# Cosformer attention and a quick-GELU MLP on one core: the first batch's chunks 0 and 1 get numerators in single PSUM banks, and w_in's first part comes as two tiles

## The chip, the core and the metric

One core of one Trainium2 chip runs the kernel. The metric is the device time of one execution in microseconds (us), the lower the better. PE is the matmul engine (TensorE; PEld are its weight loads), DVE VectorE, ACT ScalarE, POOL GpSimd, SP the sync engine. SBUF is the on-chip memory of 128 partitions, PSUM the matmul accumulator with eight banks of 512 float32 per partition.

## What is computed

Eight batches of eight heads, 576 positions and head size 64 go through a linear attention; its result, as 4608 tokens of 512 features, goes through an MLP with 2048 hidden features. All inputs are float32.

```python
phi(x) = concat([relu(x) * cos_w, relu(x) * sin_w], -1)   # 64 -> 128 features
kv  = einsum('bhsf,bhsd->bhfd', phi(k), v);  z = sum_s phi(k)
num = einsum('bhsf,bhfd->bhsd', phi(q), kv)
den = einsum('bhsf,bhf->bhs', phi(q), z) + 1e-06
x   = (num / den) as [B*S, H*D]
h   = x @ w_in;   g = h / (1 + exp(-1.702 * h));   out = g @ w_out
```

## The kernel before

The order of work on each engine is the order of the program text. Tiles come from pools, and a tile that takes over a buffer waits for the last reader of the one before it. Two PSUM pools share the eight banks: `pmm`, four single banks (name `mm`), and `pat`, two pairs of banks (name `at`). Everything below is batch 0, up to line 435; the loop over batches 1 to 7 (line 510) and the end are not touched.

**Loads.** SP loads k and q of batch 0 (lines 62 and 63). All others are issued by POOL in one queue, with a cast to bfloat16 where the tile has that type: v of batch 0 in two parts (line 132), the first two quarters of w_in (`load_win`, line 124), after POOL's own share of q the other two, then k of batch 1, two quarters of w_out (`load_wout`, line 127), q and v of batch 1 and the rest of w_out. A quarter of w_in is a tile of 512 hidden features in which feature block `fc` takes every fourth column (line 112); w_out's rows are loaded in the matching order.

**Attention of batch 0.** `trig` (line 135) makes phi of k and q on DVE, ACT and POOL. `ksum` sums phi(k) on PE, so that z is there early. `qturn_pe` (line 167) transposes phi(q) on PE into a `pmm` bank, two blocks of 64 positions at a time, and `qevac` (line 174) copies it to `qT`, on DVE or ACT. `kv_mm` (line 202) forms kv for two head pairs at a time in a `pat` pair, `kv_evac` copies it to `kvs`. Per chunk of 128 positions (four whole chunks and a half one, chunk 4) there follow:

- `num_mm` (line 226): eight matmuls, one per head, 65 columns each (64 numerators and a denominator), into a `pat` pair;
- `num_div` (line 248): DVE adds 1e-6 to the denominators, takes the reciprocal (`inv_of`) and multiplies (line 254, tile `xn`). Chunk 0 has its denominators earlier, from `den_early` (line 241) in a `pmm` bank;
- `xturn_mm` (line 269): PE transposes `xn` in four pieces into free columns of the same `pat` pair;
- `xturn_evac` (line 276): ACT copies that to `xT`, and the pair is free again.

**First product of batch 0.** `mm1_part` (line 291) multiplies w_in's block `fc` with some columns of `xT` into a `pmm` bank. For blocks 0 to 3 this is done chunk by chunk (`part`, line 414: four matmuls of 128 columns per chunk and block, "quarters" below), so that PE can begin while later chunks are still divided. After the last quarter ACT applies the four GELUs, and block 4 on runs on all 512 columns (`mm1`, line 303). The order written out by hand is lines 393 to 435: transposes of pair 3, numerators of chunks 0 and 1, transposes of pair 4, one matmul on zeros (`idle`, line 342), chunk 0's transposes, chunk 2's numerators, chunk 1's transposes, chunk 0's quarters, chunk 3's numerators, chunk 2's transposes, chunk 1's quarters, chunk 4's numerators, chunk 3's transposes, and the quarters of chunks 2 and 3. Since `pat` has two pairs, chunk 2's numerators wait for the copy of chunk 0, chunk 3's for that of chunk 1, and so on.

Of the kernel before, what the change touches and what calls it, by code (L numbers as in the profile page):

```python
# [9 lines left out]
F32 = mybir.dt.float32  # L10
BF16 = mybir.dt.bfloat16
AF = mybir.ActivationFunctionType
MUL = mybir.AluOpType.mult
# [6 lines left out]
def kernel(  # L20
# [9 lines left out]
    nc = tc.nc  # L30
    B, H, S, D = q.shape
    d_model = H * D
    d_ff = moe_w_in.shape[1]
    KC = d_model // 128
# [6 lines left out]
    one = ctx.enter_context(tc.tile_pool(name="one", bufs=1))  # L41
# [3 lines left out]
    small = ctx.enter_context(tc.tile_pool(name="small", bufs=3))  # L45
    pmm = ctx.enter_context(tc.tile_pool(name="pmm", bufs=4, space=PSUM))
# [24 lines left out]
    ident = const.tile([128, 128], BF16)  # L71
# [26 lines left out]
    qn0 = qn.rearrange("p c h f -> p (c h f)")[:, 0:NS * NI * 128].rearrange(  # L98
        "p (j i f) -> p j i f", j=NS, i=NI)
    qT = one.tile([128, H, 640], BF16, name="qT")  # L100
    w_in_sb = [one.tile([128, KC, 512], BF16, name=f"w_in{g}") for g in range(4)]
    w_out_sb = one.tile([128, FC, d_model], BF16, name="w_out_sb")
    nc.gpsimd.memset(vt[:, :, :, 64:66], 1.0)
    nc.gpsimd.memset(qT[:, :, S:640], 0.0)
# [1 line left out]

    win_r = moe_w_in.rearrange("(kc p) f -> p kc f", p=128)
    wout_r = moe_w_out.rearrange("(g p c) d -> p g c d", p=128, c=4)
    w_in_v = [t.rearrange("p k (f c) -> p k c f", c=4) for t in w_in_sb]

    def w_in_of(kc, fc):
        return w_in_v[fc // 4][:, kc, fc % 4, :]

    def load(t, src, b, eng=nc.gpsimd):
        eng.dma_start(out=t, in_=src_of(src, b))
# [5 lines left out]
                            in_=q[b, :, 512:S, :].rearrange("h p d -> p h d"))  # L121

    def load_win(g):
        nc.gpsimd.dma_start(out=w_in_sb[g], in_=win_r[:, :, ts(g, 512)])

    def load_wout(g):
        nc.gpsimd.dma_start(out=w_out_sb[:, ts(g, 4), :], in_=wout_r[:, g])

    gate = const.tile([1, 4], F32)
    nc.gpsimd.tensor_copy(gate[0:1, 0:1], kf[0:1, 0, 0:1])  # L130
    for i in (0, 2):
        nc.gpsimd.dma_start(out=vb[:, i:i + 2], in_=src_of(v, 0, i, i + 2))
    load_win(0)
    load_win(1)
    def trig(dst, src, j, act=False, eng=nc.vector):
        i = src[:, :, ts(j, 64)]
# [30 lines left out]
    def qturn_pe(c, home=None):  # L167
        tp = pmm.tile([128, 2, NI, 128], BF16, name="mm") if home is None else home
        for j in range(2 * c, min(2 * c + 2, NS)):
            for i in range(NI):  # L170
                nc.tensor.transpose(tp[:, j % 2, i], qn0[:, j, i, :], ident)  # L171
        tps[c] = tp

    def qevac(c, act=False):
        n = min(2 * c + 2, NS) - 2 * c
        o = qT[:, :, ds(c * 128, n * 64)].rearrange("f h (j p) -> f j h p", j=n)
        i = tps.pop(c)[:, 0:n].rearrange("f j i (hh p) -> f j (i hh) p", hh=2)
        if act:
            nc.scalar.activation(o, i, AF.Copy)  # L179
        else:  # L180
            nc.vector.tensor_copy(o, i)  # L181
# [10 lines left out]
    st = {}  # L192
# [9 lines left out]
    def kv_mm(i0, i1, rhs, col, n):  # L202
        for i in range(i0, i1):
            for j in range(NS):
                for hh in range(2):
                    r = slice(hh * 64, hh * 64 + 64)
                    nc.tensor.matmul(st["kv", i][:, hh, ds(col, n)], kr[r, j, i, :], rhs(r, i, j),  # L207
                                     start=(j == 0), stop=(j == NS - 1))

    def kv_evac(i0, i1, n=65):  # L210
        o = st["kvs"][:, :, i0:i1, 0:n]
        nc.vector.tensor_copy(o, st["ps", i0].rearrange("p hh (i e) -> p hh i e", e=65)[:, :, :, 0:n])  # L212
# [11 lines left out]
    nums = {}  # L224

    def num_mm(c):
        ps = pat.tile([128, 2, 512], F32, name="at")
        for h in range(H):
            i, hh = divmod(h, 2)
            nc.tensor.matmul(ps[:, h // 4, ds((h % 4) * 65, 65)], qT[:, h, ts(c, 128)],  # L230
                             st["kvs"][:, hh, i, 0:65], start=True, stop=True)
        nums[c] = [ps]

    def inv_of(d):
        den = small.tile([128, 2, 4], F32, name="den")
        nc.vector.tensor_scalar(den, d, 1e-6, None, op0=ADD)  # L236
        inv = small.tile([128, 2, 4], F32, name="inv")
        nc.vector.reciprocal(inv, den)
        return inv

    def den_early(c):
        d = pmm.tile([128, 2, 4], F32, name="mm")
        for h in range(H):
            nc.tensor.matmul(d[:, h // 4, h % 4:h % 4 + 1], qT[:, h, ts(c, 128)],
                             st["kvs"][:, h % 2, h // 2, 64:65], start=True, stop=True)
        return inv_of(d)

    def num_div(c, inv=None):
        ps = nums[c][0]
        pv = ps[:, :, 0:260].rearrange("p a (h e) -> p a h e", h=4)  # L250
        if inv is None:
            inv = inv_of(pv[:, :, :, 64])
        xn = small.tile([128, 2, 4, 64], BF16, name="xn", bufs=4)
        nc.vector.tensor_tensor(xn, pv[:, :, :, 0:64],  # L254
                                inv.unsqueeze(3).to_broadcast([128, 2, 4, 64]), op=MUL)
        nums[c].append(xn)
# [6 lines left out]
    def x_open(b):  # L263
        x[b] = xpool.tile([128, KC, MT], BF16, name="xT")

    def x_of(b, c):
        return xt[:, :, ts(b, 64)] if c == 4 else x[b][:, :, ts(c, 128)]

    def xturn_mm(c):
        ps, xn = nums[c]  # L270
        xv = xn.rearrange("p a h e -> p (a h e)")
        for kc in range(KC):
            o = ps[:, kc // 2, ds(264 + (kc % 2) * 64, 64)].bitcast(BF16)
            nc.tensor.transpose(o, xv[:, ts(kc, 128)], ident)  # L274

    def xturn_evac(b, c):
        ps = nums.pop(c)[0]
        i = ps[:, :, 264:392].bitcast(BF16).rearrange("p a (k t) -> p a k t", k=2)
        o = x_of(b, c).rearrange("p (a k) t -> p a k t", a=2)
        nc.scalar.activation(o, i, AF.Copy)  # L280

    def xturn_dma(b, c):
        xn = nums.pop(c)[1]
        n = 128 if c < 4 else 64
        nc.sync.dma_start_transpose(out=x_of(b, c), in_=xn[0:n].rearrange("p a h e -> p (a h e)"))
# [5 lines left out]
    def mm1_part(b, fc, t0, t1):  # L291
        if t0 == 0:
            hp[fc] = pmm.tile([128, MT], F32, name="mm")
        for kc in range(KC):
            nc.tensor.matmul(hp[fc][:, t0:t1], w_in_of(kc, fc), x[b][:, kc, t0:t1],  # L295
                             start=(kc == 0), stop=(kc == KC - 1))
# [12 lines left out]
    def mm1_tails(fc):  # L309
        hps = pmm.tile([128, NT], F32, name="mm")  # L310
        for kc in range(KC):
            nc.tensor.matmul(hps, w_in_of(kc, fc), xt[:, kc, :], start=(kc == 0), stop=(kc == KC - 1))  # L312
        nc.scalar.activation(gl_t[:, fc, :], hps, AF.Gelu_apprx_sigmoid)  # L313
# [28 lines left out]
    def idle(n, w=None):  # L342
        if w is None:
            w = pmm.tile([128, 512], F32, name="mm")
        for _ in range(n):
            nc.tensor.matmul(w, warm[:, 0:128], warm, start=True, stop=True)
        return w
# [34 lines left out]
    trig(qn0, qf0, 8, eng=nc.gpsimd)  # L382
    nc.gpsimd.tensor_copy(gate[0:1, 1:2], vb[0:1, 3, 0:1])
    load_win(2)
    load_win(3)
    kv_mm(0, 2, vb_rhs, 0, 64)
# [4 lines left out]
    qevac(1)  # L391
    qevac(2, act=True)
    inv0 = den_early(0)
    kv_evac(0, 2, 64)
    kv_mm(2, 4, vb_rhs, 0, 64)
    kv_evac(2, 4, 64)
    qturn_pe(3)
    qevac(3, act=True)
    num_mm(0)
    num_div(0, inv0)  # L400
    num_mm(1)
    num_div(1)
    qturn_pe(4)
    qevac(4)
    idle(1)
    x_open(0)
    xturn_mm(0)
    xturn_evac(0, 0)
    num_mm(2)
    num_div(2)  # L410
    xturn_mm(1)
    xturn_evac(0, 1)

    def part(c, *fcs):
        for fc in fcs:
            mm1_part(0, fc, c * 128, c * 128 + 128)

    part(0, 0, 1, 2, 3)
    num_mm(3)
    num_div(3)  # L420
    xturn_mm(2)
    xturn_evac(0, 2)
    part(1, 0, 1, 2, 3)
    num_mm(4)
    num_div(4)
    xturn_mm(3)
    xturn_evac(0, 3)
    xturn_dma(0, 4)
    part(2, 0, 1, 2)
    part(3, 0, 1)  # L430
    part(2, 3)
    part(3, 2, 3)
# [4 lines left out]

    load(kf, k, 1)
    load_wout(0)
    load_wout(1)  # L440
    load(qf0, q, 1)
    load(vf, v, 1)
    load_wout(2)
    load_wout(3)
    for j in range(NS):
# [137 lines left out]
```

## Time and profile before

| | us |
|---|---|
| median of 3 runs | 291.81 (291.69 to 292.36) |
| profiled execution | 292.75 |
| its span, first to last instruction | 291.0 |
| PE busy in the span | 281.8 |
| PE busy from 0 to 14 us | 10.94 of 14.00 |
| PE busy from 14.0 to 21.7 us | 6.68 of 7.70 |
| PE busy from 21.7 to 32.0 us | 10.25 of 10.30 |

The profiled execution's time is its span and 1.75 us around it. Times in what follows are us from the start of the span. In the chain of waits a row is the start, the duration and the work that the end is owed to, followed back from the last instruction; "issue" is time for which no wait shows. In a timeline a row is start, busy time, engine, line, operation, tiles, shapes and count, and in brackets the engine's idle time before it with what ended it. A matmul's duration includes its way through the array, so matmuls that follow one another start closer together than they are long; what PE is worth is read from the starts. Two views that the next section does not show: PE's waits between 13.7 and 22 us, and a table of durations there.

```profile
PEld L230 <- issue: 0.8, 1, 0.8
PE at L230 <- ACT xT L280: 0.7, 1, 0.7
PEld L274 <- DVE xn L254: 0.4, 1, 0.4
```

```profile
L254 DVE TENSOR_TENSOR xn<-at,inv 128x512 bf16<-128x512 f32 x5 | 3.5, 691 | 0.5 <-PE at L230 0.4
L280 ACT ACTIVATE xT<-at 128x512 bf16<-128x512 bf16 x4 | 2.4, 597 | 2.7 <-PE at L274 2.7
L179 ACT ACTIVATE qT<-mm 128x1024 bf16<-128x1024 bf16 x2 | 2.0, 1023 | 0.9 <-PE mm L171 0.9
```

The first lists what waited for what, in total, how often and the longest; the second gives counts, the busy sum and the mean in ns.

### The profile page before, as it was taken

What the parts mean: (1) busy time and instruction counts of PE and PEld (TensorE: products, weight loads), DVE (VectorE), ACT (ScalarE), POOL (GpSimd) and SP (SyncE); (2) the same over time, 40 slices, a digit from 0 to 9 for tenths busy, and PEclk for the clock granted to TensorE, in tenths of its full rate; (3) what the DMA queues carried; (4) which work ended last, traced back from release to release, by engine and by line L of the source; (5) the groups of instructions that cost most, each with busy time, mean ns of one, the idle gap of its engine ahead of it and who ended that gap; (6) DMA issues with size and microseconds to landing.
All of it is one profiled execution on the core that took longest, in us unless ns stands there. A gap on an engine that the chain in (4) does not pass through costs nothing.

```text
span 291.0 us, 5656 instructions
## 1 busy us (share of the span) xinstructions
PE 281.8 (97%) x2247; PEld 153.0 (53%) x2282; DVE 123.7 (43%) x356; ACT 133.1 (46%) x232; POOL 37.8 (13%) x71
## 2 busy tenths in 40 slices
PE   6989999999999999999999999999999999999995
PEld 2685475555555555555455545554555455544444
DVE  3872656912657354826582567156624200000000
ACT  6857564793157214721463136412651176751111
POOL 6560042301210011001100110011000100002000
PEclk9999999999999999999999999999999999999999
DMA  7999999982699877989797579846952600002322
GB/s 239 247 213 289 368 247 362 239 193 76 128 271 260 219 131 260 289 184 147 221 314 198 96 203 346 222 102 159 373 94 72 119 36 1 0 2 44 84 90 72
DMA packets 67770, 52.48 MB, mean 180 GB/s; under 512 B 47968, under 2 KB 57952, under 8 KB 67744
## 3 DMA queue, kind: packets, MB, share of 16 engines
q1 hardware_dynamic: 60320, 32.52, 47.0%
q0 software_dynamic: 7424, 19.60, 23.9%
q8 instruction: 18, 0.29, 0.4%
q14 instruction: 8, 0.07, 0.1%
HBM read 36.70 MB, written 9.44 MB: 159 GB/s over the span
## 4 chain that ended last, share of the span: by engine, by line
PE 91%; DMA 3%; ACT 2%; DVE 1%; issue 1%; SPq 1%; ACTq 0%
PE mm L332 42%; PE mm L295 37%; PE mm L312 5%; PE at L230 3%; PE at L207 3%; DMA qf<-in_q_dram 3%; ACT g L300 1%; PE at L274 1%; DVE qn L142 1%; DVE qT L181 0%; PE at L171 0%; ACT qT L179 0%; SPq L62 0%; DVE xn L254 0%; ACT xT L280 0%
## 5 line engine op out<-in xcount | busy, mean ns | idle before, releaser
L332 PE MATMUL mm<-w_out_sb,g 128*128 128x512 bf16 (+1 forms) x506 | 116.7, 372 | 1.3 <-issue 0.2
L295 PE MATMUL mm<-xT,w_in 128*128 128x512 bf16 (+1 forms) x551 | 111.9, 360 | 0.5
L300 ACT ACTIVATE g<-mm 128x512 bf16<-128x512 f32 x128 | 75.6, 598 | 31.0 <-PE mm L295 31.0
L295 PEld LDWEIGHTS <-w_in 128*128 128x128 bf16 x560 | 59.8, 113 | 50.9
L332 PEld LDWEIGHTS <-g 128*128 128x128 bf16 x528 | 48.6, 98 | 49.1
L336 ACT ACTIVATE ysb<-mm 128x512 f32<-128x512 f32 (+1 forms) x37 | 21.7, 586 | 105.9 <-PE mm L332 103.0
L340 POOL DMA_DIRECT2D out_dram<-ysb x39 | 21.3, 547 | 204.7 <-ACT ysb L336 204.7
L142 DVE TENSOR_SCALAR kr<-kf,cosw 128x256 bf16<-128x256 f32 x64 | 22.6, 353 | 29.4 <-DMA kf<-in_k_dram 29.4
L254 DVE TENSOR_TENSOR xn<-at,inv 128x512 bf16<-128x512 f32 x40 | 27.7, 691 | 1.9 <-PE at L230 0.4
L142 DVE TENSOR_SCALAR kr<-kf,sinw 128x256 bf16<-128x256 f32 x64 | 22.2, 347 | 0.0
L212 DVE CAST kvs<-at 128x520 bf16<-128x520 f32 (+1 forms) x9 | 5.6, 634 | 33.7 <-PE at L207 33.7
L236 DVE TENSOR_SCALAR den<-at 128x8 f32<-128x8 f32 x39 | 6.5, 166 | 31.4 <-PE at L230 31.4
L230 PEld LDWEIGHTS <-qT 128*128 128x128 bf16 x320 | 14.8, 97 | 8.8 <-issue 0.8
L230 PE MATMUL at<-kvs,qT 128*128 128x65 bf16 x320 | 16.1, 193 | 0.7 <-ACT xT L280 0.7
L155 DVE TENSOR_SCALAR qn<-qf,sinw 128x512 bf16<-128x512 f32 (+1 forms) x30 | 14.4, 480 | 0.0
L155 DVE TENSOR_SCALAR qn<-qf,cosw 128x512 bf16<-128x512 f32 (+1 forms) x30 | 14.3, 476 | 0.0
L312 PE MATMUL mm<-xt,w_in 128*128 128x512 bf16 x63 | 13.9, 379 | 0.1
L332 PE MATMUL mm<-w_out_sb,gl_t 128*128 128x512 bf16 x63 | 13.9, 379 | 0.1
L313 ACT ACTIVATE gl_t<-mm 128x512 bf16<-128x512 f32 x16 | 9.6, 597 | 4.2 <-PE mm L312 4.2
L207 PEld LDWEIGHTS <-kr 64*128 64x128 bf16 x576 | 9.3, 94 | 2.8 <-issue 2.5
L312 PEld LDWEIGHTS <-w_in 128*128 128x128 bf16 x64 | 7.2, 113 | 6.6
L332 PEld LDWEIGHTS <-gl_t 128*128 128x128 bf16 x64 | 6.3, 98 | 7.5
(63 smaller groups left out, 114.5 us busy)
## 6 DMA issues: line engine op xcount, KB each, us to landing
kf<-in_k_dram SPq DMA_DIRECT2D x5, 1152.0 KB, 6.7
vf<-in_v_dram SPq DMA_DIRECT2D x5, 1152.0 KB, 9.5
qf<-in_q_dram SPq DMA_DIRECT2D x5, 1024.0 KB, 5.9
out_dram<-ysb POOLq DMA_DIRECT2D x20, 256.0 KB, 3.9
out_dram<-ysb POOLq DMA_DIRECT2D x19, 128.0 KB, 3.2
kf<-in_k_dram POOLq DMA_DIRECT2D x2, 1152.0 KB, 11.3
vf<-in_v_dram POOLq DMA_DIRECT2D x2, 1152.0 KB, 15.7
w_in<-in_moe_w_in_dram POOLq DMA_DIRECT2D x4, 512.0 KB, 9.5
```

The costliest lines, as they stand in the source:

```text
L142: eng.tensor_scalar(o, i, 0.0, w[:, j:j + 1], op0=MAX, op1=MUL)
L155: nc.vector.tensor_scalar(o, i, 0.0, sc, op0=MAX, op1=MUL)
L207: nc.tensor.matmul(st["kv", i][:, hh, ds(col, n)], kr[r, j, i, :], rhs(r, i, j), start=(j == 0), stop=(j == NS - 1))
L230: nc.tensor.matmul(ps[:, h // 4, ds((h % 4) * 65, 65)], qT[:, h, ts(c, 128)], st["kvs"][:, hh, i, 0:65], start=True, stop=True)
L254: nc.vector.tensor_tensor(xn, pv[:, :, :, 0:64], inv.unsqueeze(3).to_broadcast([128, 2, 4, 64]), op=MUL)
L295: nc.tensor.matmul(hp[fc][:, t0:t1], w_in_of(kc, fc), x[b][:, kc, t0:t1], start=(kc == 0), stop=(kc == KC - 1))
L300: nc.scalar.activation(g, hp.pop(fc), AF.Gelu_apprx_sigmoid)
L312: nc.tensor.matmul(hps, w_in_of(kc, fc), xt[:, kc, :], start=(kc == 0), stop=(kc == KC - 1))
L313: nc.scalar.activation(gl_t[:, fc, :], hps, AF.Gelu_apprx_sigmoid)
L332: nc.tensor.matmul(yp[t, c0][:, c0:c1], w, w_out_sb[:, fc, c0:c1], start=(fc == 0), stop=(fc == FC - 1))
L336: nc.scalar.activation(ysb[:, c0:c1], yp[t, c0][:, c0:c1], AF.Identity)
L340: eng.dma_start(out=dst[:, c0:c1], in_=ysb[p0:p0 + n, c0:c1])
```

## The change

Chunks 0 and 1 have their denominators from `den_early` in one shared `pmm` bank, and their numerators, 64 columns per head, in a `pmm` bank each (`num1_mm`). DVE divides the two one behind the other (`num1_div`), PE transposes the quotients into the front half of the same bank (`x1turn_mm`) and ACT copies them from there (`x1turn_evac`). Chunks 2 and 3 so find both `pat` pairs free after kv, and their numerators come before the transposes of chunks 0 and 1. The matmul on zeros goes, the copy of pair 4 moves from DVE to ACT behind chunk 1's copy, and the quarters are interleaved otherwise: each two blocks of a chunk stand between the transposes of the chunks behind. The first quarter of w_in is two tiles of 256 columns with a DMA each, in which a block takes every second column; the first quarter of w_out is loaded in the row order that this asks for, in pieces of two rows instead of four.

```diff
@@ -98,7 +98,8 @@
     qn0 = qn.rearrange("p c h f -> p (c h f)")[:, 0:NS * NI * 128].rearrange(
         "p (j i f) -> p j i f", j=NS, i=NI)
     qT = one.tile([128, H, 640], BF16, name="qT")
-    w_in_sb = [one.tile([128, KC, 512], BF16, name=f"w_in{g}") for g in range(4)]
+    w_in0 = [one.tile([128, KC, 256], BF16, name=f"w_in0{u}") for u in "ab"]
+    w_in_sb = [one.tile([128, KC, 512], BF16, name=f"w_in{g}") for g in range(1, 4)]
     w_out_sb = one.tile([128, FC, d_model], BF16, name="w_out_sb")
     nc.gpsimd.memset(vt[:, :, :, 64:66], 1.0)
     nc.gpsimd.memset(qT[:, :, S:640], 0.0)
@@ -106,10 +107,14 @@
 
     win_r = moe_w_in.rearrange("(kc p) f -> p kc f", p=128)
     wout_r = moe_w_out.rearrange("(g p c) d -> p g c d", p=128, c=4)
+    wout0_r = moe_w_out[0:512].rearrange("(u p c) d -> p u c d", u=2, c=2)
+    w_in0_v = [t.rearrange("p k (f c) -> p k c f", c=2) for t in w_in0]
     w_in_v = [t.rearrange("p k (f c) -> p k c f", c=4) for t in w_in_sb]
 
     def w_in_of(kc, fc):
-        return w_in_v[fc // 4][:, kc, fc % 4, :]
+        if fc < 4:
+            return w_in0_v[fc // 2][:, kc, fc % 2, :]
+        return w_in_v[fc // 4 - 1][:, kc, fc % 4, :]
 
     def load(t, src, b, eng=nc.gpsimd):
         eng.dma_start(out=t, in_=src_of(src, b))
@@ -121,10 +126,17 @@
                             in_=q[b, :, 512:S, :].rearrange("h p d -> p h d"))
 
     def load_win(g):
-        nc.gpsimd.dma_start(out=w_in_sb[g], in_=win_r[:, :, ts(g, 512)])
+        if g == 0:
+            for u in range(2):
+                nc.gpsimd.dma_start(out=w_in0[u], in_=win_r[:, :, ts(u, 256)])
+        else:
+            nc.gpsimd.dma_start(out=w_in_sb[g - 1], in_=win_r[:, :, ts(g, 512)])
 
     def load_wout(g):
-        nc.gpsimd.dma_start(out=w_out_sb[:, ts(g, 4), :], in_=wout_r[:, g])
+        if g == 0:
+            nc.gpsimd.dma_start(out=w_out_sb[:, 0:4, :].rearrange("p (u c) d -> p u c d", u=2), in_=wout0_r)
+        else:
+            nc.gpsimd.dma_start(out=w_out_sb[:, ts(g, 4), :], in_=wout_r[:, g])
 
     gate = const.tile([1, 4], F32)
     nc.gpsimd.tensor_copy(gate[0:1, 0:1], kf[0:1, 0, 0:1])
@@ -239,11 +251,34 @@
         return inv
 
     def den_early(c):
-        d = pmm.tile([128, 2, 4], F32, name="mm")
+        if c == 0:
+            st["den"] = pmm.tile([128, 2, 2, 4], F32, name="mm")
+        d = st["den"][:, c]
         for h in range(H):
             nc.tensor.matmul(d[:, h // 4, h % 4:h % 4 + 1], qT[:, h, ts(c, 128)],
                              st["kvs"][:, h % 2, h // 2, 64:65], start=True, stop=True)
         return inv_of(d)
+
+    def num1_mm(c):
+        st["n", c] = pmm.tile([128, 512], F32, name="mm")
+        for h in range(H):
+            nc.tensor.matmul(st["n", c][:, ts(h, 64)], qT[:, h, ts(c, 128)],
+                             st["kvs"][:, h % 2, h // 2, 0:64], start=True, stop=True)
+
+    def num1_div(c, inv):
+        xn = small.tile([128, 2, 4, 64], BF16, name="xn", bufs=4)
+        nc.vector.tensor_tensor(xn, st["n", c].rearrange("p (a h e) -> p a h e", a=2, h=4),
+                                inv.unsqueeze(3).to_broadcast([128, 2, 4, 64]), op=MUL)
+        nums[c] = xn
+
+    def x1turn_mm(c):
+        xv = nums.pop(c).rearrange("p a h e -> p (a h e)")
+        for kc in range(KC):
+            nc.tensor.transpose(st["n", c][:, ts(kc, 64)].bitcast(BF16), xv[:, ts(kc, 128)], ident)
+
+    def x1turn_evac(b, c):
+        i = st["n", c][:, 0:256].bitcast(BF16).rearrange("p (k t) -> p k t", k=KC)
+        nc.scalar.activation(x_of(b, c), i, AF.Copy)
 
     def num_div(c, inv=None):
         ps = nums[c][0]
@@ -394,39 +429,43 @@
     kv_evac(0, 2, 64)
     kv_mm(2, 4, vb_rhs, 0, 64)
     kv_evac(2, 4, 64)
+    inv1 = den_early(1)
     qturn_pe(3)
     qevac(3, act=True)
-    num_mm(0)
-    num_div(0, inv0)
-    num_mm(1)
-    num_div(1)
-    qturn_pe(4)
-    qevac(4)
-    idle(1)
-    x_open(0)
-    xturn_mm(0)
-    xturn_evac(0, 0)
+    num1_mm(0)
+    num1_mm(1)
+    num1_div(0, inv0)
+    num1_div(1, inv1)
     num_mm(2)
     num_div(2)
-    xturn_mm(1)
-    xturn_evac(0, 1)
+    qturn_pe(4)
+    x_open(0)
+    x1turn_mm(0)
+    x1turn_evac(0, 0)
+    num_mm(3)
+    num_div(3)
+    x1turn_mm(1)
+    x1turn_evac(0, 1)
+    qevac(4, act=True)
 
     def part(c, *fcs):
         for fc in fcs:
             mm1_part(0, fc, c * 128, c * 128 + 128)
 
-    part(0, 0, 1, 2, 3)
-    num_mm(3)
-    num_div(3)
+    part(0, 0, 1)
+    part(1, 0, 1)
+    part(0, 2)
     xturn_mm(2)
     xturn_evac(0, 2)
-    part(1, 0, 1, 2, 3)
+    part(0, 3)
+    part(1, 2, 3)
+    part(2, 0, 1)
+    xturn_mm(3)
+    xturn_evac(0, 3)
     num_mm(4)
     num_div(4)
-    xturn_mm(3)
-    xturn_evac(0, 3)
     xturn_dma(0, 4)
-    part(2, 0, 1, 2)
+    part(2, 2)
     part(3, 0, 1)
     part(2, 3)
     part(3, 2, 3)
```

## The prediction

> **What bounds the kernel now.** I read the page first, then the chain of waits in the order of time, then the timeline of single engines between 12 and 22 us, then the DMA answers.
>
> ```profile
> span 291.0 us, 5656 instructions
> PE 281.8 (97%) x2247; PEld 153.0 (53%) x2282; DVE 123.7 (43%) x356; ACT 133.1 (46%) x232; POOL 37.8 (13%) x71
> PEclk9999999999999999999999999999999999999999
> ```
>
> PE is busy for 97% of the span at the full granted clock. From 16.5 us on it never pauses for more than 0.2 us: it streams 128x512 matmuls 0.216 us apart (L295 and L332, 79% of the chain). So the change can only shift the moment at which that stream begins. The chain of waits shows what sets this moment:
>
> ```profile
> 13.18 0.64 PE at L207 x36
> 13.82 0.55 PE mm L171 x8
> 14.38 0.28 PE at L230 x8
> 14.65 0.02 issue
> 14.68 0.70 DVE xn L254
> 15.38 0.05 issue
> 15.42 0.41 PE at L274 x4
> 15.84 0.02 issue
> 15.86 0.61 ACT xT L280
> 16.46 0.04 issue
> 16.51 0.40 PE at L230 x8
> 16.91 0.22 PE at L274 x4
> 17.13 0.89 PE mm L295 x16
> ...
> 20.56 0.02 issue
> 20.58 1.49 PE mm L295 x21
> ```
>
> Chunk 0 goes from its numerators (L230) through the DVE division (L254, 0.70) and the PE transposes (L274) to the ACT copy (L280, 0.61). Then PE does not start on chunk 0's product, since the next instruction in its order is chunk 2's numerators, which need the PSUM pair that this copy frees. The timeline has the two pauses:
>
> ```profile
> 15.42 0.23 PEld L274 LDWEIGHTS <-xn 128*128 128x128 bf16 x4 [0.44 <-DVE xn L254]
> 16.51 0.40 PE L230 MATMUL at<-kvs,qT 128*128 128x65 bf16 x8 [0.69 <-ACT xT L280]
> ```
>
> By starts of single matmuls PE waits 0.26 us before 15.43, 0.84 before 16.51 (the page counts 0.69, since it lets the transposes drain first) and 0.18 before 20.58, where chunk 3's copy ends last. Of the 21 matmuls from 20.58, 20 are the last quarter products and the 21st, at 21.69, opens the unbroken stream with feature block 4. **21.69 is the number to move.** From 13.76 (the transposes of pair 3) to 21.69 PE has 7.93 us: 6.65 of work and 1.28 of waiting.
>
> **The change, part by part.** From rows of this stretch: eight denominators take 0.21 (L244's eight start 0.026 apart, and the next group 0.03 behind); eight numerators 0.24; four transposes 0.23; four quarter matmuls 0.223 (16 in 0.89); a division 0.69, the next one starting 0.08 before it ends (pairs of independent DVE rows do); from the first transpose of a chunk to its ACT copy 0.43 (15.43 to 15.86; 16.75 to 17.17; 19.50 to 19.93), the copy 0.60, and 0.05 to the PE instruction that waits.
>
> 1. The denominators of chunk 1 come early: +0.21 on PE at 13.76. They need the copy of qT by DVE (L181, ends 13.38) and that DVE has read chunk 0's denominators in the shared bank (13.45): no wait. Their add and reciprocal go into DVE's idle time ahead of the division, done about 14.61.
> 2. Transposes of pair 3 at 13.97 instead of 13.76, numerators of chunk 0 at 14.43, the last drained at 14.83 (0.19 each). The division can start at 14.87 instead of 14.68, since the idle matmul and the second chunk's denominators no longer count here.
> 3. Divisions: chunk 0 to 15.56, chunk 1 from 15.48 to 16.17 (before: 16.41, behind its own add and reciprocal). PE meanwhile does the numerators of chunks 1 and 2 and the transposes of pair 4, to 15.38: 0.23 of waiting.
> 4. Chunk 0's transposes at 15.61, copy 16.04 to 16.64, **first product at 16.69** instead of 16.97, because PE now has chunk 3's numerators (a free pair) in between and nothing that waits for a copy. Chunk 1's transposes at 16.22, copy 16.65 to 17.25.
> 5. Quarter products of chunk 0, blocks 0 and 1: to 17.14; those of chunk 1 wait for its copy until 17.30 (0.16), and end 17.75; chunk 0's block 2 to 17.97.
> 6. Chunk 2's transposes at 18.00 (its division ended about 17.2), copy 18.43 to 19.03. PE has 0.67 of quarter products, to 18.90, and waits 0.18; chunk 2's blocks 0 and 1 run 19.08 to 19.53.
> 7. Chunk 3's transposes at 19.56, copy 19.99 to 20.59. PE has chunk 4's numerators and one quarter, to 20.25, and waits 0.39; the last 20 matmuls start at 20.64 instead of 20.58.
> 8. Blocks 0 to 3 end 1.11 later, as before: the stream begins at **21.75 against 21.69, +0.06 us.**
>
> Cross-check by work: 6.65 - 0.22 (the idle matmul) + 0.21 (denominators) = 6.64, and the waits are 0.23 + 0.13 (before chunk 1's transposes) + 0.24 (before 16.69) + 0.16 + 0.18 + 0.39 = 1.33: 7.97 instead of 7.93, the same within rounding. The waits are not removed; they are cut up and moved behind 16.5 us. The early half gains 0.28 us, and the shorter runs of quarters between a chunk's transposes and its products, each of which must cover 0.43 + 0.60 + 0.05 = 1.08 us, give it back.
>
> The copy of pair 4 moves from DVE (0.41) to ACT behind chunk 1's copy (about 0.60, 17.2 to 17.8). The next to wait for it are block 3's bank at 18.23 and chunk 4's numerators at 19.8: hidden. If it slipped by over 0.4 it would hold block 3.
>
> **w_in's first part in two DMAs.** Its landing, of the issue at 6.14, is
>
> ```profile
> DMA to landing us min/median/max: 9.1/9.1/9.1
> ```
>
> so 15.26, before the first use at 16.97 or 16.69: PE waited for no part of it, and half of it earlier is worth nothing. What it costs: POOL issues one DMA more (0.79 us) where it next idles 3.1 us for q; hidden. Packets halve in size. Below: by the packet records 1024-byte packets of q took 46 ns and w_in's 2048-byte reads 98, so twice 46 is no slower: 0. Above: the four w_in DMAs of equal size landed 2.5, 2.7 and once 3.45 us apart; if that 0.95 were the cost of one more DMA, all later loads shift by 0.95. I take 0.1, nearest to the packet rows. Cover: the second w_in part lands at 18.7 for a use at 21.7, the first part of w_out at 29.6 for 32.0, and q of batch 1 at 34.8, whose DVE rows end 1.7 us before PE transposes them. All of 0.95 is hidden. w_out's first part in 256 packets instead of 128 adds about 0.1 to its POOL issue; hidden by the same. Blocks 0 to 3 load weights at another stride in all eight batches: L295's loads take 113 ns and L332's contiguous ones 98, both under matmuls 216 apart: nothing either way.
>
> The Trainium skill's page "DMA: Bandwidth & Descriptors" speaks against the split: its fit gives each DMA about 2.0 us of fixed cost beside its bytes, and it advises batches of at least 1 MiB ("Bandwidth"). By that, an estimate, later loads shift by 2.0. The landings 2.5 us apart at 1 MB each do not show such a cost in a full queue.
>
> The sum is made against the profiled execution: 291.0 of span and 1.75 around it, 292.75, which is 0.94 above the median of 291.81. As a difference it holds for both: **291.81 + 0.06 = 291.9.**
>
> **The rivals.**
> - *The later waits vanish* (12%). If the copies came back sooner, PE would have from 16.69 only its work: 16 quarters 3.57, two transposes 0.46, numerators 0.24: 20.96, that is -0.73, 291.1. For: the first product does start earlier. Against: 0.43 + 0.60 + 0.05 repeats to 0.02 in four rows of before.
> - *The chain slips* (18%). ACT copies pair 3 (1.02 us, 14.63 to 15.65 by the above) ahead of chunk 0's copy at 16.04. That has 0.39 of slack; beyond it every us is one at the end, and each of four waits in a row, where before had three, passes lateness on. A slip of 0.2 at each of the four is +0.8: 292.6. Against: no such slip in the rows of before.
> - *The split stretches the loads* (5%). It decides from 1.7 us on; by 2.0 PE would wait some 0.3 at 38 us: 292.2.
> - *PE's clock falls* (5%). The idle matmul in the gap goes. At the start the first warm matmuls stand 0.43 apart and the later ones 0.22; three or four us at half speed in 14 to 22 us would cost 1.7 to 3.4, so 293.5 to 295. Against: PE's work is denser than before there, with no pause over 0.4. The page "TensorE: Matmul & The Clock Gate" of the Trainium skill, Part 1, puts the fall after an idle window of about 3.4 us; no run here shows that limit.
> - *The forecast* (60%): 291.9, itself within 291.5 to 292.3 by rounding of the rows and the spread of the three runs.
>
> Differences under 0.2% (0.58 us) are about what a measurement of this kernel can tell from none. Faster by more: 0.09, the better part of the first rival. Slower by more: 0.18, most of the second and all of the fourth. Same: 0.73. The range, 291.2 to 292.8, takes in most of the first two and the bounds of the loads.
>
> **What would show it.** In the changed profile: chunk 0's first quarter product near 16.7; its division near 14.9 and chunk 1's directly behind; no PE wait for the PSUM pair at chunk 2; instead four PE waits of 0.15 to 0.4 for ACT's copies between 16.4 and 20.7; the 128x512 stream from 21.75; w_in's first halves landed by 15.5 with no PE wait. Wrong would be: a PE wait for a DMA, ACT's copy of pair 3 ending after 16, matmuls over 0.22 apart behind 14 us, or a stream that starts before 21.2 or after 22.3.

## The result and the profile after

| | before | after |
|---|---|---|
| median, us (8 runs each, same chip) | 291.78 (291.6 to 292.36) | 292.74 (292.46 to 293.5) |
| ratio, 95% interval | | 1.0035 [1.0024, 1.0047] |
| profiled execution / its span | 292.75 / 291.04 | 293.5 / 291.79 |
| opening of the unbroken stream (block 4) | 21.69 | 22.49 |
| span behind that opening | 269.35 | 269.30 |

The changed kernel is slower by 0.96 us where 0.06 was forecast. Everything from the stream on takes the time it took, so the loss lies ahead of it. Both profiled executions lie above their medians (0.97 us before, 0.76 after), and much of that is when v and q landed. So a fairer measure than the opening itself is the time from the first kv matmul to the opening; the experiments use it. It isn't free of the loads either: in the profile of before q's last part landed at 10.64, and PE waits 0.19 us for its copy inside that stretch, where e3 below, with the same order of work and q complete at 9.35, has no such wait.

From the page of after, and then its chain of waits in the order of time (start, duration, what):

```profile
span 291.8 us, 5673 instructions
PE 283.0 (97%) x2255; PEld 151.5 (52%) x2289; DVE 123.4 (42%) x355; ACT 133.7 (46%) x233; POOL 38.7 (13%) x72
...
q8 instruction: 18, 0.29, 0.4%
```

```profile
13.74 0.28 PE mm L258 x8
14.03 0.47 PE mm L183 x8
14.50 0.25 PE mm L265 x8
14.74 0.02 issue
14.77 0.70 DVE xn L270
15.47 0.05 issue
15.52 0.41 PE mm L277 x4
15.93 0.02 issue
15.95 0.61 ACT xT L281
16.56 0.04 issue
16.60 0.27 PE mm L330 x2
16.87 0.91 issue
17.78 1.17 PE mm L330 x18
18.95 0.22 PE at L309 x4
19.17 0.67 PE mm L330 x12
...
20.73 0.61 ACT xT L315
21.33 0.04 issue
21.38 1.49 PE mm L330 x21
```

Up to 16.60 this is the chain that was forecast, link for link. Then PE does two of chunk 0's quarter matmuls (L330) and stops for 0.91 us. The row says "issue": no wait that the profile shows ended this pause. The tile that holds the weights, `xT` and the PSUM bank are those of the two matmuls before it. By starts the second quarter is at 16.66 and the third at 17.79, where 0.06 is usual: 1.07 us lost. The timeline of PE (start, busy, line, operation, count, in brackets the idle time) has it at the same place:

```profile
16.60 0.27 PE L330 MATMUL mm<-xT,w_in0a 128*128 128x128 bf16 x2
17.78 0.94 PE L330 MATMUL mm<-xT,w_in0a 128*128 128x128 bf16 x14 [0.91 <-issue]
```

Which other thing moves at that time is told by the DMA view. Cut to 15.3 to 16.4 us (queue, packets, MB, share), it has one packet of 16 KB on the queue named "instruction", in a crowd of load packets:

```profile
q0 software_dynamic: 213, 0.22, 118.5%
q8 instruction: 1, 0.02, 5.5%
```

That packet runs from 15.34 to 16.31. **The fetch theory (F in the expectations): PE has used up its instructions, and the next block of them comes late**, because the packet is asked for late and waits among POOL's loads. Number PE's records, weight loads and matmuls alike, in order from 0: the pause stands ahead of record 448 (give or take one, since some records can be missing). The page's 18 packets of 16 KB are 295 KB, and PE has 2255 + 2289 = 4544 records: 65 bytes for each, and 256 records of 64 bytes to a packet. That the queue is PE's is argued from this sum, and the trace bears it out: eight packets in a row further on start when PE has come to records 1199, 1443, 1711, 1965, 2198, 2449, 2692 and 2952, which is 233 to 268 apart. The rivals were that a handoff of the new order, or w_in's two tiles (other weights, other DMAs), cause the pause: then it stays with that part, wherever the records are counted from.

By the Trainium skill's page "Runtime: NRT & Kernel Launch" ("Instruction fetch mechanics") an engine fetches its instructions itself, in 16 KiB blocks of 256, while it works on the block before, and the fetch is mostly hidden. The 16 KB and the 256 agree with the trace; "hidden" doesn't hold here, where one fetch costs 1.07 us.

### The profile page after: what moved, and what is told of

It is laid out like the page before. It is cut to its first block, busy times and chain, and to the rows that moved or that the text cites. A ratio compares the mean times of both kernels' runs of the same rounds, so it can differ in the third digit from the quotient of the medians.

```text
span 291.8 us, 5673 instructions
## 1 busy us (share of the span) xinstructions
PE 283.0 (97%) x2255; PEld 151.5 (52%) x2289; DVE 123.4 (42%) x355; ACT 133.7 (46%) x233; POOL 38.7 (13%) x72
## 4 chain that ended last, share of the span: by engine, by line
PE 91%; DMA 4%; ACT 2%; issue 1%; DVE 0%; ACTq 0%; POOL 0%
PE mm L367 42%; PE mm L330 37%; PE mm L347 5%; PE at L219 3%; PE at L242 3%; DMA vb<-in_v_dram 2%; ACT g L335 1%; DMA kf<-in_k_dram 1%; PE at L309 0%; PE at L183 0%; ACT qT L191 0%; PE mm L183 0%; DVE qT L193 0%; DVE xn L270 0%; ACT xT L315 0%
## 5 line engine op out<-in xcount | busy, mean ns | idle before, releaser
L330 PE MATMUL mm<-xT,w_in 128*128 128x512 bf16 x377 | 83.8, 379 | 0.4
L330 PEld LDWEIGHTS <-w_in 128*128 128x128 bf16 x384 | 43.4, 113 | 39.3
L289 DVE TENSOR_TENSOR xn<-at,inv 128x512 bf16<-128x512 f32 x38 | 26.3, 691 | 1.5 <-DVE inv L250 0.2
L154 DVE TENSOR_SCALAR kr<-kf,sinw 128x256 bf16<-128x256 f32 x64 | 22.8, 356 | 0.0
L242 PEld LDWEIGHTS <-qT 128*128 128x128 bf16 x304 | 14.1, 97 | 8.0
L330 PE MATMUL mm<-xT,w_in0a 128*128 128x512 bf16 (+1 forms) x87 | 15.6, 320 | 1.3 <-issue 0.9
L330 PE MATMUL mm<-xT,w_in0b 128*128 128x512 bf16 (+1 forms) x87 | 15.6, 320 | 0.1
L242 PE MATMUL at<-kvs,qT 128*128 128x65 bf16 x304 | 15.4, 193 | 0.0
L330 PEld LDWEIGHTS <-w_in0a 128*128 128x128 bf16 x88 | 7.6, 98 | 8.3 <-issue 1.6
```

The source lines that it names most:

```text
L154: eng.tensor_scalar(o, i, 0.0, w[:, j:j + 1], op0=MAX, op1=MUL)
L289: nc.vector.tensor_tensor(xn, pv[:, :, :, 0:64], inv.unsqueeze(3).to_broadcast([128, 2, 4, 64]), op=MUL)
```

## The experiments

Times are medians; the ratio is to the kernel before, measured beside it, with its 95% interval. In the table "record" is the start of that record and "packet" the start and end of the 16 KB packet. "Pause" is what PE loses by starts at record 448, and "stage" the time from the first kv matmul to the stream's opening in the profile. Record 192 is one block of 256 ahead of record 448.

| | record 192 | packet | record 448 | pause | stage |
|---|---|---|---|---|---|
| before | 11.69 | 14.97-15.95 | 17.89 | none | 10.31 |
| after | 11.94 | 15.34-16.31 | 17.79 | 1.07 | 10.86 |
| after, again | 11.22 | 14.66-15.64 | 17.02 | 1.06 | 10.81 |
| e2 order alone | 11.12 | 14.45-15.42 | 16.73 | 0.84 | 10.62 |
| e3 split alone | 11.08 | 14.58-15.56 | 16.88 | 0.1 | 10.03 |
| e4 12 records more | 11.32 | 14.86-15.84 | 17.27 | 1.6 | 11.60 |
| e1 160 more | 7.34 | 10.39-11.37 | 14.14 | none | 9.90 |
| e5 126 more | 7.43 | 9.83-10.81 | 13.81 | none | 9.90 |
| e7 126 more, on before | 7.48 | 9.90-10.87 | 13.84 | none | 9.92 |
| e6 = e5, turns early | 7.47 | 9.39-10.37 | 13.77 | none | 9.51 |
| e11 turns early | 11.46 | 14.83-15.80 | 17.26 | 1.05 | 10.25 |
| e8 w_in late | 11.03 | 11.91-12.87 | 16.54 | none there | waits for w_in |
| e9 half of w_in early | 11.14 | 12.86-13.84 | 15.94 | none | 10.92 |
| e10 = e9, turns early | 11.53 | 12.88-13.86 | 16.33 | none | 9.52 |
| e13 POOL freed | 11.28 | 12.94-13.92 | 16.04 | none | 9.93 |
| e12 = e13, turns early | 10.92 | 12.97-13.94 | 15.71 | none | 9.50 |
| e14 before, POOL freed | 11.06 | 12.98-13.95 | 16.91 | none | 9.95 |
| e15 = e12, loads later | 11.07 | 12.89-13.86 | 15.85 | none | 9.99 |

(e9 and e15 include 0.78 and 0.33 us of waiting for w_in.)

**The two parts alone.** e2 is the change with one w_in tile and one DMA, e3 the kernel before with the two tiles of w_in.

> The changed kernel with w_in's first part in one tile and one DMA again: the new order alone. The PE rows are the same in number. Theory F: the pause of 0.9 to 1.1 us stays ahead of PE row 448 and the time is 292.5 to 292.9. Theory S: no pause, 291.7 to 292.0. Theory O: as F.

> The kernel before with w_in's first part in two tiles and nothing else: the split alone. Theory F and theory O: no pause beyond those of before, 291.7 to 292.0. Theory S: 292.4 to 292.8, with a PE wait at the first quarter product.

e2: 292.46 us, 1.0025 [1.0014, 1.0035]. e3: 291.83, 1.0005 [0.9996, 1.0013]. From PE's timeline of e2:

```profile
15.78 0.27 PE L318 MATMUL mm<-xT,w_in 128*128 128x128 bf16 x2
16.73 1.17 PE L318 MATMUL mm<-xT,w_in 128*128 128x128 bf16 x18 [0.68 <-issue]
```

The pause is there without the split, at the same count of matmuls; the split alone costs nothing. With both the time is 0.28 larger than with the order alone and the pause 0.22 to 0.23; the intervals of the two times overlap. In e2 record 448 follows record 192 by 5.61 us, in after by 5.85 and 5.80.

**The same kernel once more** repeats the pause in an execution whose v landed earlier.

> The changed kernel once more, for a second profile: the first one was 0.76 us above the median, with kv's matmuls waiting for v until 11.6 us. Theory F: kv's matmuls may start near 10.8 instead, and the pause before row 448 is there all the same, 0.9 to 1.2 us, ending 5.6 to 6.0 us behind row 192. Rival (the pause belongs to that slow execution): under 0.3 us.

292.74 us; 1.06 us between the same two matmuls. So the pause is no accident of one execution.

**Records moved.** Six small matmuls on zeros (12 records) at the start, then 80 (160 records):

```diff
     w = idle(12)
+    for _ in range(6):
+        nc.tensor.matmul(w[:, 0:2], warm[:, 0:128], warm[:, 0:2], start=True, stop=True)
```

> The changed kernel with 6 tiny matmuls (12 PE rows) behind the twelve on zeros. Theory F: the pause moves up in the program by 12 rows, with the row number 448: it stands before the first transposes of chunk 1 (about 16.1) instead of between the second and third quarter matmul, and ends again 1.2 to 1.7 us after the end of the 16 KB instruction packet, near 17.6; the time stays 0.6 to 1.2 above the kernel before. Theories S and O: the pause stays between the second and third quarter matmul.

> The changed kernel with 80 tiny matmuls (128x2, 160 PE rows with their weight loads) behind the twelve matmuls on zeros, where PE waits for k. Theory F (PE ran out of instructions: the trace of the changed kernel has a 0.9 to 1.1 us pause with no wait named ahead of PE row 448, 16.7 to 17.8 us, 1.5 us after a 16 KB packet on the instruction queue): the rows move row 448 to kv's second half near 13.4 us and the request for it to before 6 us, so the pause near 16.7 goes, the stream of 512-column matmuls opens near 21.6 instead of 22.5, and the time is 291.7 to 292.0 (0.997 of the changed kernel). Theory S (w_in's split) and theory O (a wait in the new order, for a bank or a copy, that the profile does not name): the pause stays where it is in the program, 292.6 to 292.9.

e4: 293.72 us (one run). The pause has moved 12 records up, to chunk 1's transposes:

```profile
15.22 0.41 PE L242 MATMUL at<-kvs,qT 128*128 128x65 bf16 x8
17.26 0.38 PE L277 MATMUL mm<-ident,xn 128*128 128x128 bf16 x4 [1.64 <-DVE inv L250]
```

The row names a DVE reciprocal as what ended the pause. That can't be: the quotients which these transposes read were complete at 15.53, PE had loaded the first of them as weights at 15.58, and the reciprocals near by, for chunks 2 and 3, were done at 15.84 and 16.87. Nothing else in the kernel was changed, and the pause stands where the count puts it. It is longer than in after because PE comes to it sooner and the packet doesn't. This is the experiment that tells the theory from both rivals: the pause follows the number of the instruction, not the work, the weights or the tile. It also says to mistrust a named releaser that had long been done.

e1: the packet comes at 10.39, and there is no pause. The time is a miss all the same: 293.84, 1.0076 [1.0063, 1.0089]. The 80 matmuls of two columns kept PE issuing but not at full speed: the 512-column matmuls behind them took 0.59 us, the mean granted clock is 0.993 instead of 1.0, and q's transposes come late. The first load of v was complete only at 12.40 as well (10.66 in e3; the same in e5 below), and kv starts at 12.52.

**Records moved at full clock.** e5 puts 72 matmuls of 64 columns in the place of nine of the twelve 512-column ones (126 records more in about the same time); e7 does the same to the kernel before.

```diff
-    w = idle(12)
+    w = idle(3)
+    for _ in range(72):
+        nc.tensor.matmul(w[:, 0:64], warm[:, 0:128], warm[:, 0:64], start=True, stop=True)
```

> The changed kernel with nine of the first twelve 512-column matmuls on zeros cut into 72 of 64 columns: the same columns for PE, 126 more rows in its program, all in its first 5 us. The runs so far say: the packet with rows 448 on starts 3.0 to 3.5 us behind the start of row 192, and PE gets past row 448 no earlier than 5.6 to 5.95 us behind row 192. With 126 rows more, row 192 lies near 7.5 us and row 448 among the last kv matmuls, near 13.6. Theory F: no pause, the stream of 512-column matmuls opens at 21.5 to 21.8, 291.7 to 292.0. Rival (the pause only moves, since PE's rows are too dense anywhere): a pause of over 0.5 us before row 448 or row 704, 292.4 or more.

> The kernel before with the same cut of the matmuls on zeros, as a control. It has no pause at row 448 that counts (row 448 comes 6.2 us behind row 192). Theory F: 291.6 to 291.9, no change over 0.2. Rival (the cut itself makes the kernel faster or slower, by clock or start): a change of over 0.4 either way.

e5: 292.84 us, 1.0036 [1.0023, 1.0049], a miss: no pause, and still slow. e7: 292.76, 1.0036 [1.0023, 1.0048]. The control explains the miss: the edit itself costs the kernel before 1.04 us. The packet, now early, runs while v is landing, and v lands late. Of the 16 parts in which the first load of v reports, half were there at 10.43 (10.44 in e3), but the last at 11.89 (10.66), and kv, which waits for it, starts at 11.93 (10.78). That the packet holds up this last part is argued from such rows (e1 and e6 have the same), not tried by itself. Read against each other, e5 and e7 say what the order is worth where neither pauses: +0.08 us, and stages of 9.90 and 9.92.

**Transposes moved ahead of the quarters.** e11 is the change with the transposes of chunks 2 and 3 earlier, e6 is that order in e5.

```diff
     part(0, 0, 1)
-    part(1, 0, 1)
-    part(0, 2)
     xturn_mm(2)
     xturn_evac(0, 2)
+    part(1, 0, 1)
+    part(0, 2)
+    xturn_mm(3)
+    xturn_evac(0, 3)
     part(0, 3)
...
```

> The changed kernel with the transposes of chunks 2 and 3 moved up, loads and zeros as in the changed kernel. Theory F: the pause before row 448 stays (0.9 to 1.1 us), the waits for ACT's copies behind it shrink by 0.4 to 0.6: 292.1 to 292.4. Rival (the copies, not the pause, set the end): 291.2 or less.

> As the one before, and the transposes of chunks 2 and 3 moved up, ahead of quarters that are ready: chunk 2's behind the first two quarters, chunk 3's behind chunk 0's block 2, so that ACT's copies lie beside quarters of PE. By the prediction's rows the waits of 0.16, 0.18 and 0.39 us go and the stream opens near 21.1 instead of 21.69: 291.0 to 291.4, below the kernel before by 0.4 to 0.8. Rival (what the copies cost comes back elsewhere, at the GELUs or at a pause before row 704): 291.6 to 292.0.

e11: 292.17, 1.001 [1.0002, 1.0019], 0.57 below after's median, as F has it: the pause stays (1.05), but the waits behind it are shorter, and the stage is 10.25 instead of 10.81 to 10.86. e6: 292.45, 1.002 [1.0011, 1.0029], a miss in the time, again by v's landing; against e5 the stage is 0.39 shorter.

**Loads moved out of the packet's way.** If the packet waits for the loads queued ahead of it, fewer of these should bring it sooner. e8 issues both early parts of w_in only behind POOL's wait for v; e9 leaves the first half tile early and puts the rest there, and it also loads w_out's first part ahead of k of batch 1; e10 is e9 with e11's order. From e9:

```diff
-    load_win(0)
-    load_win(1)
+    nc.gpsimd.dma_start(out=w_in0[0], in_=win_r[:, :, ts(0, 256)])
...
     nc.gpsimd.tensor_copy(gate[0:1, 1:2], vb[0:1, 3, 0:1])
+    nc.gpsimd.dma_start(out=w_in0[1], in_=win_r[:, :, ts(1, 256)])
+    load_win(1)
```

> The changed kernel with the first two parts of w_in issued behind POOL's gate near 13.1 us, with the other two, so that the load queue is empty from about 13 to 15. What the 3.4 us between row 192 and its packet are made of: if it is a queue behind the loads, the packet starts by 13.5 to 14.5 and PE passes row 448 by 16.7 if w_in is there; if it is a fixed time of the request, the packet starts 3.0 to 3.5 behind row 192 as before. The first quarter product may now wait for w_in, so the total time tells nothing.

> The changed kernel in which only the first half of w_in's first part is issued early; the second half and w_in's second part are issued behind POOL's gate near 13 us with the rest, and w_out's first part ahead of k of batch 1. Theory F with a queue (the packet with PE's rows from 448 on stands behind the loads: 3.4 us behind row 192 with w_in queued, 0.9 with an empty queue): the queue ends near 13.1, the packet starts by 13.2, no pause over 0.3 us before row 448, 291.4 to 291.8, under the changed kernel by 0.9 to 1.3. Rival (the loads that come later now make PE wait, for w_in's second half or w_out's first part): a PE wait for a DMA between 16 and 32 us, 292.2 or more.

> As e9, and the transposes of chunks 2 and 3 moved up as in e6: both edits that the readings ask for. Stream of 512-column matmuls 0.4 to 0.6 us earlier than in the kernel before: 291.1 to 291.4. Rival: a pause of PE's rows or a wait for w_in's second half eats it, 291.7 to 292.2.

e8: 295.3 us (one run). The packet starts 0.88 us behind record 192, against 3.3 to 3.5 with the loads queued. There is no pause at record 448, but PE waits for w_in until 16.41 and so comes there late; what e8 shows is the packet. e9: 293.91, 1.006 [1.004, 1.0081], and e10: 294.34, 1.0076 [1.0058, 1.0093]. Both miss in the time: no pause, a packet 1.35 to 1.72 behind record 192, but the loads behind the hole are late. PE's waits in e9 from 15 to 45 us:

```profile
PE mm L329 <- DMA w_in<-in_moe_w_in_dram: 0.8, 1, 0.8
PE at L182 <- DVE qn L153: 0.6, 1, 0.6
```

Half of the 16 parts of that load of w_in were there at 18.90, but the last at 21.70, for a use at 20.96; batch 1's q was complete at 38.27. The second row is only a part of what q costs. By starts of matmuls PE loses 1.66 us in e9 ahead of the transposes of batch 1's q, and 0.93 in e10, whose q was complete at 36.50; with q complete at 34.6 to 34.8 (after again, e12, e14) it loses nothing there. e10's profile is of its fastest execution, 292.82; that its others lose still more in this way is not shown.

**The hole made small.** e13 issues the early parts of w_in as e9 does, but POOL no longer makes phi of q's last block (ACT does), and its wait is for v's first part, so that the loads behind the hole start sooner. e14 is the same in the kernel before (with the split), e12 is e13 with e11's order, e15 is e12 waiting for v's second part.

What e13 has beside that:

```diff
-    trig(qn0, qf0, 8, eng=nc.gpsimd)
-    nc.gpsimd.tensor_copy(gate[0:1, 1:2], vb[0:1, 3, 0:1])
+    nc.gpsimd.tensor_copy(gate[0:1, 1:2], vb[0:1, 1, 0:1])
...
     qevac(2, act=True)
+    trig(qn0, qf0, 8, act=True)
```

> The changed kernel in which ACT does POOL's share of phi(q) (pair 4, behind the copy of pair 2), so that POOL issues the second half of w_in's first part and all later loads behind v's first part, near 11 us. Theory F: the packet with rows 448 on starts near 13 instead of 14.7, no pause over 0.3 before row 448, no PE wait for a load: 291.6 to 292.0. Rival (the packet waits as long as before, since loads are queued again by then): pause 0.8 to 1.1, 292.5 or more.

> The kernel before with the split and the same freeing of POOL, as a control. Its rows from 192 to 448 take about 5.8 us anyway: 291.6 to 291.9 by theory F. Rival (moving POOL's share to ACT or the later issue costs by itself): 292.2 or more.

> As e13, with the transposes of chunks 2 and 3 moved up. Theory F: 0.4 to 0.6 below e13, 291.1 to 291.5, faster than the kernel before. Rival: the pause stays, 292.1 to 292.4, as e11.

> As e12, with the gate on v's second part: the second half of w_in's first part is issued near 12.3. Theory F: no pause; a hole of some 0.7 us in the load queue, which PE's next uses cover: 291.1 to 291.6. Rival (as in e9 the loads behind the hole come 2 us late and PE waits for w_in's second part or q of batch 1): 292 or more.

| | us | ratio |
|---|---|---|
| e13 | 292.0 | 1.0008 [0.9995, 1.0021] |
| e14 | 292.06 | 1.0019 [1.0001, 1.0036] |
| e12 | 291.69 | 0.9995 [0.9978, 1.0011] |
| e15 | 294.41 | 1.0082 [1.0067, 1.0097] |

e13's DMA view from 12.9 to 14 us has the packet 2.4 us sooner than after had it, among packets of w_in's halves (v had landed at 12.33):

```profile
q0 software_dynamic: 313, 0.16, 121.4%
q8 instruction: 1, 0.02, 5.5%
```

and its timeline runs the quarters through, 16 in a row from 15.94, where after stopped behind the second:

```profile
15.94 1.20 PE L329 MATMUL mm<-xT,w_in0a 128*128 128x128 bf16 x16
16.98 0.39 PE L329 MATMUL mm<-xT,w_in0b 128*128 128x128 bf16 x4
```

With no pause the order is worth what was forecast, next to nothing: the stages of e13 and e14 are 9.93 and 9.95, and their times differ by -0.06 us, within intervals that are wider than that. e12 has the shortest stage, 9.50, and is the best version found; it is level with the kernel before and not shown to be faster. The runs of e12, e13 and e14 spread by 1.9 to 2.6 us (e12 from 291.28 to 293.86), those of the kernel before by 1.26. A part of this is seen in e13's profile, an execution of 292.58: batch 1's q was complete only at 36.25, and PE loses 0.53 us by starts ahead of its transposes. What makes q late in some executions was not tried. e15 misses: its loads behind POOL's wait are issued 1.56 us later than e12's (w_in's second half at 12.31 against 10.75), w_out's first part is complete 3.28 us later (32.82 against 29.54), and PE waits 1.6 us for it. The waits from 15 to 45 us:

```profile
PE mm L366 <- DMA w_out_sb<-in_moe_w_out_dram: 1.6, 1, 1.6
PE mm L329 <- DMA w_in<-in_moe_w_in_dram: 0.3, 1, 0.3
```

## Why the prediction was wrong

1. **Steps 1 to 4 held.** Chunk 1's denominators took 0.22 (0.21 forecast); the divisions ran from 14.77 to 16.06, 1.29 for both (14.87 to 16.17); the copy for chunk 0 began at 15.95 (16.04), and the first product at 16.60 (16.69). Chunk 1's transposes were at 16.11 (16.22).
2. **Step 5 failed.** It has PE run chunk 0's blocks 0 and 1, eight quarters, straight to 17.14. PE ran two and lost 1.07 us at record 448. The cross-check by work has the same gap: "6.64" of work and "1.33" of waits assume that PE always has its next instruction. The likeliest case had no such mechanism in it, and neither did a rival. The stream opened at 22.49, beyond the 22.3 that the prediction gave as a sign of being wrong.
3. **Steps 6 and 7 held as differences.** From chunk 2's transposes to its copy 0.42, a copy of 0.60, a wait of 0.18 ahead of the next quarters (0.18 forecast); for chunk 3 0.39 (0.39). The wait of 0.16 for chunk 1's copy went under in the pause. So the forecast opening with these differences is 21.75 + 1.07 - 0.16 - 0.09 (the first product's lead) = 22.57 against 22.49 measured; 0.08 stays as rounding.
4. **Why the new order runs dry and the old one hardly.** With the loads queued, record 448 started 5.6 to 5.95 us behind record 192, and never sooner (e2, e3, e4, e11, after): 3.3 to 3.5 until the packet starts, 0.97 for the packet, 1.3 to 1.5 until PE goes on. The old order needs about that long by itself, 5.85 in e14, where the packet came early (5.80 in e3, 6.20 in the profile of before), since some 0.84 us of waiting for chunk 0's copy falls into the stretch. The prediction saw that these waits are "cut up and moved behind 16.5 us"; behind 16.5 is behind record 448. Without the pause PE would have reached that record after 4.78 us (4.76 in e13, which has no pause), and the fetch took their place as the wait, with the moved waits still to come.
5. **The split.** "I take 0.1", hidden: right by itself, +0.05 us. w_in's halves landed at 14.33 and 15.71 with no PE wait. The assumption "twice 46 is no slower" was off: the halved packets took 60 ns against 98 for the whole ones, and w_in's first part occupied the engines for 3.84 us instead of 3.14, summed over packets and divided by 16. Beside the new order this may matter: with the split, record 448 comes 5.80 to 5.95 behind record 192, in e2, one execution without it, 5.61. That the longer occupation is the cause of the 0.28 us between e2 and after is argued from these rows, not tried by itself.
6. **The rivals.** The later waits did not vanish. The chain did not slip: ACT's copy of pair 3 ended at 15.56, 0.39 ahead of chunk 0's copy, which is the slack that was forecast. The clock did not fall: quarters behind the pause stand 0.056 apart as before. The time lies in the range, and near the 292.6 of the slipping chain, by luck, since it comes from a mechanism that none of them named; "slower by more" than 0.2% had a chance of 0.18 for other reasons. e12 shows that the first rival's gain was partly to be had by another order: its stage is 0.43 below that of e13.

What stays open: why PE needs another 1.3 to 1.5 us from the end of the packet to its next matmul (no record shows what lies between), and how the packet waits. By the Trainium skill's page "DMA: Bandwidth & Descriptors" ("Queues, rings and completion order") each DMA engine takes turns between its queues, a packet of typically 9 to 17 descriptors at a time. If the profile's rows of 60 and 98 ns are such descriptors, one turn takes 0.5 to 1.7 us, an estimate, and by that alone the instruction packet would not wait 3.4 us behind another queue's loads; with the page's ceiling of 64 descriptors (3.8 to 6.3 us, an estimate too) it could. No row here shows the turns. The runs show the lag shrink with the loads queued (0.88 with none of w_in, 1.35 to 2.05 in the six with half a tile, 3.3 to 3.5 with all; 1.9 to 3.05 in e1 and e5 to e7, where the packet came while v was landing) and not why.

## What to carry to other kernels

A pause on "issue" that no wait explains may be the engine's own instructions: count its records to the pause, add a few harmless ones ahead, and see whether it moves. An order that packs many short instructions into a busy stretch of loads brings the next block's boundary nearer; waits taken out ahead of a boundary buy nothing if the fetch sets the pace, only less work behind it does. Judge an order against a control in which the same side effects stand (e5 with e7, e13 with e14), since edits at the start of a kernel move its loads by more than the effect that was looked for.

## What the runs showed of the hardware

- A block of PE's instructions is one packet of 16 KB that takes 0.97 us here. In the four profiles where it ran while v was landing, the last of that load's 16 parts came 1.4 to 1.9 us behind the middle one (e1, e5, e6 and e7), against 0.2 in e3. If the packet is the cause it isn't the only one: in after's profiled execution v's last part was 1.2 us behind with no such packet near.
- The next block cost nothing here: with 512-column matmuls 0.216 us apart it took PE 15.5 us from record 448 to record 704 in after (17.79 to 33.29), and the packet had come at 21.47.
- Many tiny matmuls did not hold PE's speed (e1: 512-column matmuls of 0.59 us behind 80 of two columns).
- Behind a gap in POOL's queue of loads the last part of a load came later than the rest. Of w_out's first load, issued 1.56 us later in e15 than in e12, the middle part came 0.82 us later (29.44 against 28.62) and the last 3.28 us later (32.82 against 29.54). Why one part falls so far behind stays open.
